# An attention and mixture-of-experts kernel: a new order for VectorE inside a unit, accumulators kept over the groups, and later stores of x from twelve buffers

## The chip, the cores and the metric

The kernel runs on one NeuronCore of a Trainium2 chip. The metric is the device time of one execution in microseconds. TensorE (PE) multiplies matrices into PSUM, VectorE (DVE) and ScalarE (ACT) read and write PSUM and SBUF, GpSimd (POOL) converts data and issues the loads of weights, and SyncE (SP) issues the other DMAs from one queue. Every engine takes its instructions in the order in which they were written and waits for the others through semaphores.

## What is computed

The first part is attention with a sliding window, for 8 batches of 576 positions and 8 heads of 64:

```python
scores = scale * np.matmul(q, k.transpose(0, 1, 3, 2))
mask = (rel >= 0) & (rel < 128)
scores = np.where(mask, scores + slopes * -np.abs(rel), -1e9)
attn = softmax(scores)
x = (attn @ v)            # as 4608 tokens of 512 values
```

The second part routes the 4608 tokens over 8 experts. Eight rounds of row and column normalization of exp(x @ w_gate) give a weight P for every token and expert, and every expert works on every token:

```python
for e in range(8):
    h = np.maximum(x @ w1[e], 0.0)          # 512 -> 1024
    out += P[:, e:e+1] * (h @ w2[e])        # 1024 -> 512
```

## The kernel before, in words

**Stage one** (to about 366 us) does the attention batch by batch, together with experts 0 and 1. A batch has five blocks of positions (four of 128, one of 64), and a block two steps of four heads. A step computes scores on TensorE, exponentials on ScalarE (`exps`, L429), the mask on VectorE (L442) and the weighted values on TensorE (`values`, L467); VectorE divides by the sum and writes half of a block of x into the tile `xsb` (L478). `turn_x` transposes the finished block, on TensorE for batches 0, 1, 2 and 7 (L498, copied out at L507 or L509) and by a DMA for the others (L511), and then stores the block to the DRAM tensor `xd` (L512), which stage two reads. The `xsb` tiles come from 3 buffers, which the converted tail of q and k (`turn_tail`) shares. The loads of v (`load_v`, L373), of the next batches' q and k (`load_qk`, L270) and the stores stand on SP's one queue in the order of the program. For batches 0 to 2, q and k are converted (L286, L288; L284 on GpSimd) and turned on TensorE in pairs of heads (`turn_pe`, L350). A filler weaves matmuls of experts 0 and 1 (L115 and L137) between the steps, so many per step as a backlog asks; their results go to the DRAM tensor `ysp`.

**Stage two** does experts 2 to 7 for 18 groups of 256 tokens. A unit is one expert for one group, 108 in all. Both matrix products are cut into 2x2 blocks. In most units the first product takes seven block products instead of eight, as Strassen's method does: TensorE runs the parts a11, s1, s2, a12, s3, s4, a22 (`part`, L957) into three PSUM banks A, B and C. ScalarE copies one bank into another between the parts (L1109, L1110, L1115), VectorE adds two pairs of sums, here called h3 (L1121) and h1 (L1125), and ScalarE applies the maximum with zero (`relu`, L970). Part a22 writes bank B again and so comes after h3 has read it. Part s1 reads T1, s2 reads T2, s3 reads T3 and a22 reads T4, which are sums of x blocks that VectorE makes one unit ahead (`sums_x`, L902 to L904) from the transposed tile `xset`. Expert 7, and the units before the fifth, take the plain first product (`l1_bank`, L937, L946).

The x of a unit is scaled by P two units ahead (`scale_x`, L878) and transposed by two DMAs on SP (`turn_xs`, L890) that land in `xset`.

The second product of unit n-1 runs inside unit n, between the parts of the first: seven products numbered 1 to 7 (`product`, L995), which need sums of h that VectorE makes at the head of unit n (`make_sums`, L974 to L976). They accumulate over the experts of a group in two PSUM tiles of two banks each: products 3, 4 and 5, 2 in the first, 6, 7 and 1 in the second. When a group's last expert is through, VectorE adds the products into the SBUF tile `acc` (`gather`, L1037): 3 and 4 as soon as they are done, 5 and 2 later in the same unit, and 6, 7 and 1 at the head of the next unit, whereupon `finish` (L1045) stores the output. The results of experts 0 and 1 of the next group are loaded into `y` (`load_y`, L1006) and start `acc` (`begin`, L1010 and L1013) three and four units into the group.

"First unit" below is the unit in which the old group's last products run, "second unit" is the next one.

## Time and profile before

| | us |
|---|---|
| median of 3 runs | 1111.12 (1110.44 to 1112.74) |
| the profiled execution | 1110.26 |
| its span | 1108.3 |
| TensorE busy | 1022.0 (92%) |
| VectorE busy | 768.7 (69%) |
| ScalarE busy | 557.0 (50%) |
| stores of x | 32 of 128 KB, 8 of 64 KB |

The rows of the profile read as follows. A row in order of time has its start, its length, the engine, the line of the kernel, the operation, output and inputs with their sizes and a count of merged instructions. In brackets stands the idle time of the engine before it and what ended that. PEld rows are loads of weights for the matmuls. A row of waits has the engine and line that waited, what it waited for, the total, how often and the longest. Busy time of TensorE is modelled at the ends of its matmuls.

### The profile page before, as it was taken

The numbers are of one execution on the slowest core, as the hardware profiler recorded it, in microseconds if no ns is written. First come the engines' busy times: TensorE is split into PE (matmuls) and PEld (weight loads), VectorE is DVE, ScalarE is ACT, GpSimd is POOL, SyncE is SP. The second block draws the span as 40 slices with busy tenths as digits, with TensorE's granted clock in tenths as the row PEclk, the third lists the DMA queues.
The fourth block names the chain that finished last, engine by engine and source line by source line (L and its number), as shares of the span: only waits on it lengthen the run. The fifth ranks groups of instructions, "written<-read, shape, count | busy, mean of one in ns | idle before, by whom it ended". The sixth has DMA issues, their size and how long they took to land.

```text
span 1108.3 us, 26671 instructions
## 1 busy us (share of the span) xinstructions
PE 1022.0 (92%) x11079; PEld 806.6 (73%) x11079; DVE 768.7 (69%) x1720; ACT 557.0 (50%) x973; POOL 80.8 (7%) x143
## 2 busy tenths in 40 slices
PE   6589899999999999999999899999999999989988
PEld 4344444444544789888889888888888988888977
DVE  4355565666578697776877776877776877777866
ACT  6346445554433345555555555555555555545543
POOL 1210323125110000000000000000000000000000
PEclk9699999999999999999999999999999999999999
DMA  9982787889997323324422432332332332342361
GB/s 250 208 221 56 197 180 197 187 216 178 225 188 143 91 49 86 82 51 81 93 62 66 89 77 50 87 77 54 82 77 52 90 78 54 87 78 49 87 115 30
DMA packets 264424, 122.37 MB, mean 110 GB/s; under 512 B 201968, under 2 KB 255728, under 8 KB 264304
## 3 DMA queue, kind: packets, MB, share of 16 engines
q1 hardware_dynamic: 249568, 102.68, 40.1%
q0 software_dynamic: 14304, 17.84, 9.7%
q8 instruction: 86, 1.41, 0.5%
q14 instruction: 34, 0.28, 0.1%
q10 hardware_dynamic: 432, 0.16, 0.1%
HBM read 78.30 MB, written 23.59 MB: 92 GB/s over the span
## 4 chain that ended last, share of the span: by engine, by line
PE 46%; DVE 27%; DMA 5%; ACT 5%; issue 4%; SPq 1%; DVEq 0%; ACTq 0%
PE psS_m L995 12%; PE psh L115 8%; PE psy L137 8%; PE psh L937 6%; DVE acc L1037 5%; PE psB L957 4%; DMA xset<-xs 4%; DVE hs L1121 4%; DVE hs L974 4%; ACT hs L970 4%; DVE hs L975 3%; DVE xs L878 3%; PE psA L957 2%; DVE xset L902 2%; PE psC L957 2%
## 5 line engine op out<-in xcount | busy, mean ns | idle before, releaser
L995 PEld LDWEIGHTS <-hs 128*128 128x128 f16 x2996 | 280.2, 98 | 49.6 <-issue 22.2
L957 PEld LDWEIGHTS <-w1l 128*128 128x128 f16 x2720 | 174.2, 98 | 37.7 <-issue 34.1
L970 ACT ACTIVATE hs<-hs 128x512 f16<-128x512 f16 x170 | 104.3, 630 | 189.3 <-DVE hs L1121 189.3
L995 PE MATMUL psS_m<-w2l,hs 128*128 128x256 f16 x1440 | 186.6, 273 | 1.1 <-DVE acc L1037 0.8
L974 DVE TENSOR_TENSOR hs<-hs 128x1024 f16<-128x1024 f16 x107 | 74.0, 691 | 133.5 <-ACT hs L970 80.3
L115 PE MATMUL psh<-xT,w1t 128*128 128x512 f16 (+1 forms) x608 | 142.3, 373 | 4.1 <-DVE xT L509 3.7
L137 PE MATMUL psy<-w2t,hT 128*128 128x512 f16 x576 | 136.0, 383 | 2.8 <-DVE xsb L478 2.8
L127 ACT ACTIVATE hT<-psh 128x512 f16<-128x512 f32 (+1 forms) x144 | 83.5, 586 | 107.9 <-PE psh L115 107.5
L995 PE MATMUL psS_m<-more,hs 128*128 128x256 f16 x864 | 119.3, 275 | 0.0
L957 PEld LDWEIGHTS <-s 128*128 128x128 f16 x1632 | 106.2, 98 | 3.2
L946 ACT ACTIVATE hs<-psh 128x512 f16<-128x512 f32 x92 | 54.9, 597 | 99.9 <-PE psh L937 97.6
L957 PE MATMUL psA<-xset,w1l 128*128 128x128 f16 x1360 | 104.6, 220 | 0.0
L137 PEld LDWEIGHTS <-hT 128*128 128x128 f16 x576 | 53.8, 98 | 64.8 <-issue 3.1
L115 PEld LDWEIGHTS <-w1t 128*128 128x128 f16 x608 | 55.6, 100 | 57.0 <-issue 8.7
L546 DVE CAST yo<-psy 128x512 f16<-128x512 f32 x68 | 46.8, 689 | 59.6 <-PE psy L137 58.8
L429 ACT ACTIVATE pt<-psS 128x1024 f16<-128x1024 f32 (+2 forms) x80 | 67.7, 852 | 37.4 <-PE psS L411 30.8
L957 PE MATMUL psB<-xset,s 128*128 128x128 f16 x1088 | 82.9, 219 | 0.0
L1115 ACT COPY psC<-psB 128x512 f32<-128x512 f32 x85 | 48.5, 571 | 59.8 <-PE psB L957 59.8
L957 PE MATMUL psB<-xset,w1l 128*128 128x128 f16 x680 | 52.1, 220 | 26.6 <-DVE hs L1121 26.5
L1037 DVE TENSOR_TENSOR acc<-acc,psS_m 128x256 f32<-128x256 f32 (+1 forms) x162 | 74.1, 504 | 3.4 <-PE psS_m L995 2.8
L442 DVE TENSOR_TENSOR pt<-pt,mask 128x1024 f16<-128x1024 f16 (+2 forms) x80 | 53.3, 666 | 32.4 <-ACT pt L429 32.2
L937 PE MATMUL psh<-xset,w1t 128*128 128x256 f16 x576 | 74.7, 273 | 0.0
(113 smaller groups left out, 1414.3 us busy)
## 6 DMA issues: line engine op xcount, KB each, us to landing
y<-ysp SPq DMA_DIRECT2D x36, 256.0 KB, 3.2
ysp<-yo SPq DMA_DIRECT2D x68, 128.0 KB, 3.0
v<-in_v_dram SPq DMA_DIRECT2D x32, 256.0 KB, 4.4
out_dram<-acc SPq DMA_DIRECT2D x31, 256.0 KB, 2.6
q<-in_q_dram SPq DMA_DIRECT2D x5, 1024.0 KB, 7.3
k<-in_k_dram SPq DMA_DIRECT2D x5, 1024.0 KB, 9.7
xtok<-xd SPq DMA_DIRECT2D x34, 128.0 KB, 2.2
w2t<-in_moe_w_dram POOLq DMA_DIRECT2D x4, 1024.0 KB, 11.1
```

The lines of the kernel that those rows point to most:

```text
L115: nc.tensor.matmul(out=ps[:, 0:nt], lhsT=w1ts[e][:, dt, P * ft : P * ft + P], rhs=xT[:, at : at + nb, dt, :], start=(dt == 0), stop=(dt == ...
L127: nc.scalar.activation(out=st["hT"][:, ft, 0:nt], in_=ps[:, 0:nt], func=AF.Relu)
L137: nc.tensor.matmul(out=ps, lhsT=st["hT"][:, ft, P * ms : P * ms + P], rhs=w2ts[e][:, ft, :], start=(ft == 0), stop=(ft == NFT - 1),)
L429: nc.scalar.activation(out=pt[0:nk, :, 0 : nk + nn], in_=ps[0:nk, :, :, 0 : nk + nn].rearrange("p a y n -> p (a y) n"), func=AF.Exp, scale ...
L442: nc.vector.tensor_tensor(out=pt[0:nk, :, 0:w], in0=pt[0:nk, :, 0:w], in1=mask[0:nk, hs, 0:w], op=ALU.mult)
L937: nc.tensor.matmul(out=ps[:, f, :], lhsT=W1L[e][:, dt, P * ft : P * ft + P], rhs=x[:, dt], start=(f == 0 and dt == 0), stop=(dt == NDT - 1 ...
L946: nc.scalar.activation(out=h[n][:, fh : fh + 2, j : j + 2, :].rearrange("p t f k -> p f t k"), in_=ps.rearrange("p f (t k) -> p f t k", t= ...
L957: nc.tensor.matmul(out=ps[:, j, :], lhsT=SL[e][w][:, k, P * j : P * j + P], rhs=xset[n % 2][:, x, P * k : P * k + P], start=(start and j = ...
L970: nc.scalar.activation(out=h[n][:, slot], in_=src, func=AF.Relu)
L974: nc.vector.tensor_tensor(out=t[:, 4:6], in0=t[:, 0:2], in1=t[:, 2:4], op=ALU.add)
L995: nc.tensor.matmul(out=Ms[g, bk][:, half, :], lhsT=h[n][:, LEFT[m], f, :], rhs=W2L[e][RIGHT[m]][:, f, :], start=(e == 2 and f == 0 and hal ...
L1037: nc.vector.tensor_tensor(out=a, in0=a, in1=p2, op=op)
```

## The change

In stage one, `xsb` has 12 buffers (`XSB`) instead of 3. `turn_x` no longer stores its block at once: it appends it to a list, and `keep_x(3)` stores the block of three turns before; the rest is stored after the last turn.

In stage two:
- The two accumulator tiles are made once and serve all groups (`Ms[bk]` instead of `Ms[g, bk]`).
- In a unit with seven parts, bank B is named before bank C, the copy of A into B stands ahead of part s1, and product 3 runs before s1, product 4 after it.
- VectorE makes `sums_x` after h3 and h1, no longer before them.
- In the first unit the gather of 5 and 2 comes after those sums, ahead of products 6 and 7 in the program.
- In the second unit products 6 and 7 are gathered after the sums of h, and product 1 only after h1.
- `finish` and `load_y` come at the end of the unit, behind `turn_xs` on SP's queue.

```diff
-    XPE, YO = 3, 6
+    XPE, YO, XSB = 3, 6, 12
...
-                xsbs[b, kb] = asb.tile([P, H, Dh], FP16, name=f"xsb_{b}_{kb}", tag="xsb", bufs=3)
+                xsbs[b, kb] = asb.tile([P, H, Dh], FP16, name=f"xsb_{b}_{kb}", tag="xsb", bufs=XSB)
...
+        kept: list = []
+
+        def keep_x(left=0):
+            while len(kept) > left:
+                blk, lo, nk, xsb = kept.pop(0)
+                nc.sync.dma_start(out=xd[blk, lo : lo + nk, :], in_=xsb[0:nk].rearrange("p h d -> p (h d)"))
...
-            nc.sync.dma_start(out=xd[blk, lo : lo + nk, :], in_=xsb[0:nk].rearrange("p h d -> p (h d)"))
+            kept.append((blk, lo, nk, xsb))
+            keep_x(3)
...
         turn_x(B - 1, NKB - 1)
+        keep_x()
...
-                if e == 2 and half == 0 and bk % 2 == 0:
-                    t = aps.tile([P, 2, 2, 2 * P], FP32, name=f"psS_m{g}_{bk}", tag="psS", bufs=2)
-                    Ms[g, bk], Ms[g, bk + 1] = t[:, 0], t[:, 1]
+                if not bk % 2 and bk not in Ms:
+                    t = aps.tile([P, 2, 2, 2 * P], FP32, name=f"psS_m{bk}", tag="psS", bufs=2)
+                    Ms[bk], Ms[bk + 1] = t[:, 0], t[:, 1]
...
         for n in range(N):
+            end = ends(n - 1)
+            done, late = late, ()
             if n > 0:
                 make_sums(n - 1)
-            if late:
-                gather(units[n - 2][0], *late)
-                finish(units[n - 2][0])
-                late = []
...
+            if done:
+                gather(units[n - 2][0], 6, 7)
             scale_x(n + 2)
-            if n > 0 and units[n - 1][1] == 2:
-                load_y(g)
...
                 part(n, pa, "a11", B11, True)
+                pb = bank(n, "B")
+                nc.scalar.copy(out=pb, in_=pa)
+                product(n - 1, 3)
                 pc = bank(n, "C")
                 part(n, pc, "s1", T1, True)
-                pb = bank(n, "B")
-                nc.scalar.copy(out=pb, in_=pa)
                 nc.scalar.copy(out=s5, in_=pc)
-                product(n - 1, 3, 4)
+                product(n - 1, 4)
                 if end:
                     gather(g, 3, 4)
...
                 part(n, pb, "s3", T3)
-                sums_x(n + 1)
                 nc.vector.tensor_tensor(out=h[n][:, 3], in0=pb, in1=s5, op=ALU.add)
                 relu(n, 3, h[n][:, 3])
                 part(n, pc, "s4", B22)
                 turn_xs(n + 2)
                 nc.vector.tensor_tensor(out=h[n][:, 1], in0=pc, in1=s5, op=ALU.add)
                 relu(n, 1, h[n][:, 1])
+                if done:
+                    gather(units[n - 2][0], 1)
+                sums_x(n + 1)
+                if end:
+                    gather(g, 5, 2)
                 product(n - 1, 6, 7)
                 part(n, pb, "a22", T4)
                 relu(n, 2, pb)
                 product(n - 1, 1)
-                if end:
-                    gather(g, 5, 2)
-                    late = (6, 7, 1)
...
+            if done:
+                finish(units[n - 2][0])
+            if n > 0 and units[n - 1][1] == 2:
+                load_y(g)
+            if end:
+                late = (6, 7, 1)
```

More of the change, by code (lines that the diff above doesn't have):

```diff
@@ L316, in turn_tail @@
         def turn_tail(b):
-            t16 = asb.tile([P, HD], FP16, name=f"t16_{b}", tag="xsb", bufs=3)
+            t16 = asb.tile([P, HD], FP16, name=f"t16_{b}", tag="xsb", bufs=XSB)
             nc.gpsimd.tensor_copy(out=t16, in_=tails.pop(b).rearrange("p h d -> p (h d)"))
@@ L990, in product @@
                 bk, half = BANK[m]
-                if e == 2 and half == 0 and bk % 2 == 0:
-                    t = aps.tile([P, 2, 2, 2 * P], FP32, name=f"psS_m{g}_{bk}", tag="psS", bufs=2)
-                    Ms[g, bk], Ms[g, bk + 1] = t[:, 0], t[:, 1]
+                if not bk % 2 and bk not in Ms:
+                    t = aps.tile([P, 2, 2, 2 * P], FP32, name=f"psS_m{bk}", tag="psS", bufs=2)
+                    Ms[bk], Ms[bk + 1] = t[:, 0], t[:, 1]
                 for f in range(NF2):
                     nc.tensor.matmul(
-                        out=Ms[g, bk][:, half, :],
+                        out=Ms[bk][:, half, :],
                         lhsT=h[n][:, LEFT[m], f, :],
@@ L1021, in gather @@
                 bk, half = BANK[m]
-                ps = Ms[g, bk][:, half, :]
+                ps = Ms[bk][:, half, :]
                 for lo, step, op in {
@@ L1082 @@
         xs[:] = [per.tile([P, HD], FP16, name=f"xs_{i}", tag="yo", bufs=YO) for i in range(4)]
-        late: list = []
+        late: tuple = ()
         for n in range(N):
             g = units[n - 1][0]
+            end = ends(n - 1)
+            done, late = late, ()
             if n > 0:
                 make_sums(n - 1)
-            if late:
-                gather(units[n - 2][0], *late)
-                finish(units[n - 2][0])
-                late = []
             some((4, 1, 0, 3, 2)[n] if n < 5 else 0)
@@ L1094 @@
                 quads_w1(units[n - 1][1])
+            if done:
+                gather(units[n - 2][0], 6, 7)
             scale_x(n + 2)
-            if n > 0 and units[n - 1][1] == 2:
-                load_y(g)
             if n > 0 and units[n - 1][1] in (4, 5):
                 begin(g, units[n - 1][1] - 4)
-            end = ends(n - 1)
             if strassen(n):
@@ L1130 @@
                 product(n - 1, 1)
-                if end:
-                    gather(g, 5, 2)
-                    late = (6, 7, 1)
-            else:
+            else:
+                if done:
+                    gather(units[n - 2][0], 1)
                 pairs = ((3, 4), (5, 2), (6, 7), (1,))
@@ L1140 @@
                         gather(g, *pairs[i])
-                    if i == 2:
-                        sums_x(n + 1)
                 turn_xs(n + 2)
-                if end:
-                    late = (6, 7, 1)
+                sums_x(n + 1)
+            if done:
+                finish(units[n - 2][0])
[3 more added lines that the diff above has]
+                late = (6, 7, 1)
             if n == N - E + 2:
```

## The prediction

> **What bounds the kernel now.** I read the page first, then busy time by stretches, then the list of waits, and only then the order of time where the long waits lie. The page's span, the stretches before and after 366 us (where the dense experts end), and three rows of waits (the two of TensorE are those after 430 us, the one of VectorE is of the whole span):

> ```profile
> span 1108.3 us, 26671 instructions
> ```
> ```profile
> 0.00:366.00 366.00, 331.35 (x2563) 170.47 (x2564) 214.41 (x494) 175.78 (x286) 79.97 (x142) 0.97 0.86 187
> 366.00:1108.30 742.30, 690.60 (x8518) 636.14 (x8515) 554.33 (x1226) 381.26 (x687) 0.87 (x1) 1.00 0.33 73
> ```
> ```profile
> PE psB L957 <- DVE hs L1121: 26.1, 41, 3.3
> PE psS_m L995 <- DVE acc L1037: 18.3, 17, 1.1
> ```
> ```profile
> DVE xsb L478 <- DMA xd<-xsb: 33.8, 6, 17.5
> ```

> The columns of the stretches are length, then busy time of PE, PEld, DVE, ACT and POOL. TensorE is busy 331.35 of 366.00 and 690.60 of 742.30 us, so it is the bound in both, and only its idle 34.7 and 51.7 us can be won. The 51.7 has two names: 41 waits of part a22 for the sum h3 (26.1 us), and 17 waits of 1.1 us, one at each change of group. The chain of waits names the same lines. In stage one VectorE waits for the store of an x block to free its buffer.

> **The x stores and the twelve buffers.** Rows picked from stage one in order of time, and two loads by their time to landing (issued between 20 and 30 us):

> ```profile
> 18.74 2.72 SPq L270 DMA_DIRECT2D k<-in_k_dram  x1
> 28.33 0.88 POOL L100 DMA_DIRECT2D w2t<-in_moe_w_dram  x1
> 29.55 1.19 SPq L512 DMA_DIRECT2D xd<-xsb  x1
> ...
> 39.82 0.61 POOL L383 CAST v<-v 128x512 f16<-128x512 f32 x1 [7.62 <-DMA v<-in_v_dram]
> 40.16 0.42 DVE L478 TENSOR_TENSOR xsb<-psN,rden 128x256 f16<-128x256 f32 x1 [17.50 <-DMA xd<-xsb]
> ...
> 50.10 0.81 PE L350 MATMUL psT<-ident,c 128*128 128x128 f16 x8
> 57.82 0.39 PE L467 MATMUL psN<-v,pt 128*128 128x65 f16 x7 [0.95 <-DVE pt L442]
> 59.14 1.04 PE L137 MATMUL psy<-w2t,hT 128*128 128x512 f16 x4
> ...
> 73.32 0.42 DVE L478 TENSOR_TENSOR xsb<-psN,rden 64x256 f16<-64x256 f32 x1 [2.14 <-DMA xd<-xsb]
> ...
> 127.09 3.54 PE L137 MATMUL psy<-w2t,hT 128*128 128x512 f16 x8 [2.79 <-DVE xsb L478]
> ...
> 148.16 1.89 PE L137 MATMUL psy<-w2t,hT 128*128 128x512 f16 x8
> ...
> 168.00 1.02 ACT L429 ACTIVATE pt<-psS 128x1024 f16<-128x1024 f32 x1
> 170.75 0.30 PE L467 MATMUL psN<-v,pt 128*128 128x65 f16 x4 [2.33 <-DVE pt L442]
> ```
> ```profile
> w2t<-in_moe_w_dram POOLq DMA_DIRECT2D x1, 1024.0 KB, 11.1
> k<-in_k_dram SPq DMA_DIRECT2D x1, 512.0 KB, 11.1
> ```

> With three buffers the fourth x block waits for the first block's store, which stands on SP's queue behind the loads of the next batch: VectorE stands 17.50 us, and everything behind it. With twelve the fourth block takes a fresh buffer; the store is issued three turns later, so v loads and the loads of batch 2 pass it on SP, and nothing waits for it.

> What is late next? The second half of k for batch 1: issued until 18.74 + 2.72 = 21.46, landing 11.1 later at 32.6; with its cast and copy (0.8) the third pair of turns can start at 33.4. Today it starts at 50.10: a gain of 16.7. The next loads are in time on that schedule: w2t lands at 28.33 + 0.88 + 11.1 = 40.3 and is first needed at 59.14 - 16.7 = 42.4; the second v block of batch 1 is cast at 39.82 (0.61 long), and the values that read it start at 57.82 - 16.7 = 41.1. Margins of 1 to 2 us, so I bound this term by 17.5 above and by 2 below (the DMA engines are full there, and only the three 128 KB stores leave the early queue: 384 KB at the stage's 187 GB/s, the last column above); I take 16.7, as the rows of the loads reach it.

> The other waits of this kind: 2.1 at 73.32. At 127.09 TensorE's 2.8, and eight matmuls that then took 3.54 instead of 1.89 (1.6 more): 4.4. At 170.75 TensorE waited 2.33, but ScalarE's exponentials came only at 168.00, so I take 1.0. After 180 us TensorE is busy throughout, and an advance is carried on. The same forty stores are issued on SP, the last three together behind the final turn. **Stage one: 16.7 + 2.1 + 4.4 + 1.0 = 24.2 us less.**

> **The order inside a unit.** One change of group today. The first unit of the new group still gathers products 3, 4, 5, 2 of the old one; the second gathers 6, 7, 1. Rows picked from the order of time, the last two from the unit after:

> ```profile
> 488.82 1.28 DVE L1037 TENSOR_TENSOR acc<-acc,psS_m 128x512 f32<-128x512 f32 x2
> 490.16 1.03 PE L995 MATMUL psS_m<-w2t,hs 128*128 128x256 f16 x8 [1.10 <-DVE acc L1037]
> ...
> 491.03 0.61 PE L957 MATMUL psB<-xset,s 128*128 128x128 f16 x8
> 491.74 0.69 DVE L1121 TENSOR_TENSOR hs<-psB,s5s 128x512 f16<-128x512 f32 x1 [0.65 <-PE psB L957]
> 492.35 0.68 DVE L1125 TENSOR_TENSOR hs<-psC,s5s 128x512 f16<-128x512 f32 x1
> 492.95 1.41 DVE L1037 TENSOR_TENSOR acc<-acc,psS_m 128x256 f32<-128x256 f32 x4
> 493.68 0.61 PE L957 MATMUL psA<-xset,w1l 128*128 128x128 f16 x8
> 494.27 0.69 DVE L974 TENSOR_TENSOR hs<-hs 128x1024 f16<-128x1024 f16 x1
> ...
> 497.32 0.61 DVE L878 TENSOR_SCALAR xs<-xtok,L_sb 128x512 f16<-128x512 f16 x2
> 497.85 0.42 DVE L902 TENSOR_TENSOR xset<-xset 128x512 f16<-128x512 f16 x1
> 498.10 1.04 PE L995 MATMUL psS_m<-w2l,hs 128*128 128x256 f16 x8
> 498.84 0.68 DVE L1121 TENSOR_TENSOR hs<-psB,s5s 128x512 f16<-128x512 f32 x1
> 499.57 0.61 PE L957 MATMUL psB<-xset,w1l 128*128 128x128 f16 x8 [0.43 <-DVE hs L1121]
> ...
> 505.18 0.42 DVE L902 TENSOR_TENSOR xset<-xset 128x512 f16<-128x512 f16 x1 [1.60 <-DMA xset<-xs]
> 506.98 0.61 PE L957 MATMUL psB<-xset,w1l 128*128 128x128 f16 x8 [1.07 <-DVE hs L1121]
> ```

> What it wins: the sums of x (497.85 to 498.84, 0.99 us, and at 505.18 a wait of 1.60 for a transpose) no longer stand before h3. Then h3 starts 0.71 after part s3 (491.03 to 491.74), before products 6 and 7 are through, and a22 never waits. The sums, now behind h1, are done before the next unit's T1 and T2 are read, and the transposes no longer stand behind two stores and two loads on SP. All 26.1 us go. A wait is longer than its bracket says: products 6 and 7 take 0.87, so 498.10 + 0.87 = 498.97, and a22 started at 499.57, 0.17 later than the 0.43 accounts for; times 41 that is 7.0. Two of the waits, the 3.3 of that row and one of 2.26, also halved the clock for a while (below, 1.6 each): 3.2. Together 36.3.

> What it does not win: the 18.3. In the built program product 5 still waits for the gather of 3 and 4, because both lie in one two-bank tile; keeping the tile over the groups changes its name and not that wait. The gather stands where it stood: 1.1 us times 17 stay.

> What it costs: two waits move onto the queue ahead of TensorE. In the built program product 3 of the new group waits for the last instruction of the gather of 5 and 2, and product 6 for the gather of 1. Today both are over in time. In the changed order:
> - The gather of 5 and 2 stands behind the sums: 492.95 + 0.99 = 493.94, plus 1.41 is 495.35. Product 3 now comes before s1, ready at 493.68 + 0.45 = 494.13, and starts 0.06 after the gather (490.10 to 490.16 above) at 495.41: a stall of 1.28.
> - Six blocks later (3, s1, 4, s2, a12, 5 and 2: 3.09) s3 starts at 498.50, h3 at 499.21, h1 at 499.82, the gather of 1 at 500.42, done after 0.64 at 501.06. Product 6 is ready at 499.39 and starts at 501.12: a stall of 1.73.

> TensorE works in order, so nothing behind these is done meanwhile. 3.01 us times 17 changes of group: 51.2. **Stage two: 51.2 - 36.3 = 14.9 us more.** From both sides: if a reused tile lets these products go at once, nothing is paid; if the clock falls, 27 more.

> The rest moves without cost: ScalarE's copy of psA goes ahead of that of psC (same count); stores of the output and loads of y go behind the transposes on SP, and y is read two units later.

> **Stalls and the clock.** Three rows of TensorE after stalls, and the granted clock (the number before the last two of the stretch) behind the second:

> ```profile
> 409.22 1.03 PE L995 MATMUL psS_m<-w2t,hs 128*128 128x256 f16 x8 [1.65 <-DVE acc L1037]
> ...
> 792.41 0.83 PE L957 MATMUL psB<-xset,w1l 128*128 128x128 f16 x8 [2.26 <-DVE hs L1121]
> ...
> 796.70 0.61 PE L957 MATMUL psB<-xset,s 128*128 128x128 f16 x8
> ```
> ```profile
> 793.50:795.00 1.50, 1.50 (x14) 1.38 (x13) 0.86 (x2) 0.61 (x3) 0.00 (x0) 0.50 0.00 0
> ```

> After 1.65 us of idling the matmuls kept their speed (eight in 1.03); after 2.26 the granted clock was 0.50, and a22 to s2 took 4.29 instead of the 2.66 that their blocks sum to: 1.6 lost. The new stall of 1.73 lies between, nearer to the harmless row, so I count nothing.

> [...]

> **The rivals.**
> - Slower: the clock. If the stall of 1.73 trips it, as the one of 2.26 did, each costs 1.6: at half of the changes of group 1101 + 14 = 1115, at all of them 1128. It decides from about 6 of 17 on. For it: two stalls in each such unit; against it: 1.65 was harmless.
> - Slower: the front is bound by its loads. If w2t or v come later than the rows say, the 16.7 shrinks towards 2: 1116. For it: POOL waited 7.62 for v at 39.82; against it: stores leave that queue.
> - The sums still wait for late transposes, and s1 waits where a22 did: half of the 36.3 remains, 1119.
> - The change does what its words say, and accumulators kept by bank free TensorE at the change of group: the 51.2 is not paid, 1050. The built program's waits speak against it.

> **How the numbers follow.** The profiled run took 1110.26, its span 1108.3 and 2.0 around it; that is 0.1% under the median of 1111.12. 1110.26 - 24.2 + 14.9 = 1101. Its own range is 1095 to 1108. Chances: this case 0.50, the clock 0.15, the front 0.12, late transposes 0.10, no stalls at the change of group 0.05, something else 0.08. For 8 in 10 the range runs from 1095 to 1120. Within 0.2% (2.2 us, about what three runs can tell, since they spread over 0.2%) I put 0.10; faster 0.56; slower 0.34.

> **What would show it.** Right: VectorE's wait for xd gone, the third pair of turns near 33 us and stage one over near 342; waits of psB gone; waits of psS_m grown from 18 to about 70 us, three at each change of group, of 1.1, 1.3 and 1.7; second units of 9.2 us and others of 6.2. Wrong: a granted clock below 1.00 behind the stalls, waits of PE for v or w2t before 60 us, waits of psC for the sums, or psS_m waiting no longer than today.

## The result, and the profile after

The changed kernel takes 1101.16 us (median of 4 runs) against 1110.84 us before, a ratio of 0.9918 with a 95% interval of 0.9892 to 0.9944: 0.8% faster. The forecast was 1101.0. The profiled execution took 1100.92 us, its span 1098.3, against 1110.26 and 1108.3.

The small difference is made of two large ones. Here are the two stages of the changed kernel (stretch, then busy time of PE, PEld, DVE, ACT and POOL, granted clock, DMA share, GB/s); stage two begins at 340.7 us, where its first matmul starts:

```profile
0.00:340.70 340.70, 326.64 (x2563) 168.51 (x2564) 212.65 (x494) 175.40 (x286) 78.08 (x142) 1.00 0.92 201
340.70:1098.30 757.60, 685.47 (x8517) 634.77 (x8515) 555.80 (x1226) 392.78 (x687) 0.88 (x1) 1.00 0.32 71
```

Before, stage two began at 366.1 us and lasted 742.2. So stage one is 25.4 us shorter and stage two 15.4 us longer; forecast were 24.2 and 14.9. (Ten traces below have the same first stage as the changed kernel; in them stage two begins between 339.8 and 344.3 us, so the 25.4 is known to a few us only.) TensorE was idle for 51.7 us of stage two before, and is for 72.1 now.

The list of waits, stage two alone (engine, line, what was waited for, total, times, longest):

```profile
PE psS_m L1004 <- DVE acc L1046: 66.4, 52, 1.9
```

No row of psB waiting for h3 is left: the 41 waits of 26.1 us are gone. Those of the products grew from 19.9 us in 18 waits, over the same stage, to 66.4 in 52, and there are three at each change of group instead of one. Here is one change of group in order of time, TensorE first (the last row is the next change of group), then VectorE:

```profile
467.29 1.03 PE L1004 MATMUL psS_m<-w2t,hs 128*128 128x256 f16 x8 [1.09 <-DVE acc L1046]
...
472.53 0.60 PE L1004 MATMUL psS_m<-more,hs 128*128 128x256 f16 x4 [1.11 <-DVE acc L1046]
...
478.27 1.03 PE L1004 MATMUL psS_m<-w2l,hs 128*128 128x256 f16 x8 [1.60 <-DVE acc L1046]
...
509.04 1.03 PE L1004 MATMUL psS_m<-w2t,hs 128*128 128x256 f16 x8 [1.09 <-DVE acc L1046]
```
```profile
470.86 0.29 DVE L913 TENSOR_TENSOR xset<-xset 128x256 f16<-128x256 f16 x1
471.07 1.41 DVE L1046 TENSOR_TENSOR acc<-acc,psS_m 128x256 f32<-128x256 f32 x4
...
476.94 0.68 DVE L1131 TENSOR_TENSOR hs<-psC,s5s 128x512 f16<-128x512 f32 x1
477.54 0.68 DVE L1046 TENSOR_TENSOR acc<-acc,psS_m 128x512 f32<-128x512 f32 x1
```

The three stalls are those of products 5, 3 and 6. Product 3 starts right behind the gather of 5 and 2 (471.07 + 1.41 = 472.48, start 472.53), which now stands behind the sums of x; product 6 starts right behind the gather of 1 (477.54 + 0.68 = 478.22, start 478.27), which stands behind h1. From one change of group to the next it is 509.04 - 467.29 = 41.75 us every time.

In stage one the gates' matmuls (x @ w_gate, L518 before and L526 after) make good marks, because the same sets come in the same places of both kernels. The kernel before, then the changed one, in order of time:

```profile
41.59 1.48 PE L248 MATMUL psJ<-ones 128*128 128x256 f16 x6
42.88 4.76 PE L115 MATMUL psh<-xT,w1t 128*128 128x256 f16 x32
...
60.25 0.54 PE L518 MATMUL psG<-wg_sb,xT 128*128 128x8 f16 x16
...
112.25 0.55 PE L518 MATMUL psG<-wg_sb,xT 128*128 128x8 f16 x16
...
132.53 1.02 PE L115 MATMUL psh<-xT,w1t 128*128 128x512 f16 x4 [0.54 <-DVE xT L509]
...
149.88 0.55 PE L518 MATMUL psG<-wg_sb,xT 128*128 128x8 f16 x16
...
171.57 1.89 PE L115 MATMUL psh<-xT,w1t 128*128 128x512 f16 x4
...
183.05 0.55 PE L518 MATMUL psG<-wg_sb,xT 128*128 128x8 f16 x16
...
216.82 0.55 PE L518 MATMUL psG<-wg_sb,xT 128*128 128x8 f16 x16
```
```profile
24.19 0.82 PE L248 MATMUL psJ<-ones 128*128 128x256 f16 x6
24.84 3.66 PE L115 MATMUL psh<-xT,w1t 128*128 128x256 f16 x32
...
31.20 0.61 PE L350 MATMUL psT<-ident,c 128*128 128x128 f16 x8
...
41.12 0.54 PE L526 MATMUL psG<-wg_sb,xT 128*128 128x8 f16 x16
...
91.00 0.55 PE L526 MATMUL psG<-wg_sb,xT 128*128 128x8 f16 x16
...
108.08 1.02 PE L115 MATMUL psh<-xT,w1t 128*128 128x512 f16 x4 [1.95 <-DVE xT L516]
...
125.43 0.55 PE L526 MATMUL psG<-wg_sb,xT 128*128 128x8 f16 x16
...
145.54 0.30 PE L467 MATMUL psN<-v,pt 128*128 128x65 f16 x4 [1.67 <-DVE pt L442]
...
156.64 0.55 PE L526 MATMUL psG<-wg_sb,xT 128*128 128x8 f16 x16
...
182.51 0.30 PE L467 MATMUL psN<-v,pt 128*128 128x65 f16 x4 [0.97 <-DVE pt L442]
...
191.55 0.55 PE L526 MATMUL psG<-wg_sb,xT 128*128 128x8 f16 x16
```

The lead of the changed kernel is 19.1 us at the first mark, 21.3 at the second, 24.5 at the third, 26.4 at the fourth (183.05 against 156.64) and 25.3 at the last: a new wait at 182.51 takes 1.1 back. (VectorE still has two waits for an x store in its list, 2.4 us in all, but at the tile yo.) Nothing waits for a store of x any more in front of the fourth block, and the third pair of turns starts at 31.20 instead of 50.10.

### The profile page after: what moved, and what is told of

Its sections match the earlier page's. It is cut to its first block, busy times and chain, and to the rows that moved or that the text cites. A ratio compares the mean times of both kernels' runs of the same rounds, so it can differ in the third digit from the quotient of the medians.

```text
span 1098.3 us, 26710 instructions
## 1 busy us (share of the span) xinstructions
PE 1012.1 (92%) x11079; PEld 803.3 (73%) x11079; DVE 768.4 (70%) x1720; ACT 568.2 (52%) x973; POOL 79.0 (7%) x143
## 3 DMA queue, kind: packets, MB, share of 16 engines
q8 instruction: 86, 1.41, 0.5%
## 4 chain that ended last, share of the span: by engine, by line
PE 65%; DVE 15%; issue 1%; ACT 1%; DMA 0%; DVEq 0%; SPq 0%
PE psS_m L1004 25%; PE psB L966 9%; PE psy L137 6%; PE psh L115 6%; PE psh L946 6%; DVE acc L1046 5%; PE psC L966 5%; PE psA L966 5%; DVE hs L1131 2%; DVE hs L1127 1%; DVE hs L983 1%; DVE hs L984 1%; DVE xs L887 1%; ACT hs L955 1%; DVE hs L985 1%
## 5 line engine op out<-in xcount | busy, mean ns | idle before, releaser
L1004 PEld LDWEIGHTS <-hs 128*128 128x128 f16 x2996 | 277.0, 98 | 97.8 <-issue 72.8
L1004 PE MATMUL psS_m<-more,hs 128*128 128x256 f16 x864 | 129.0, 273 | 18.8 <-DVE acc L1046 18.8
L983 DVE TENSOR_TENSOR hs<-hs 128x1024 f16<-128x1024 f16 x107 | 74.0, 691 | 101.0 <-ACT hs L955 53.6
L115 PE MATMUL psh<-xT,w1t 128*128 128x512 f16 (+1 forms) x608 | 139.7, 368 | 3.4 <-DVE xT L516 3.0
L137 PE MATMUL psy<-w2t,hT 128*128 128x512 f16 x576 | 134.3, 380 | 0.0
L1127 DVE TENSOR_TENSOR hs<-psB,s5s 128x512 f16<-128x512 f32 x85 | 58.8, 692 | 81.1 <-PE psB L966 79.8
L137 PEld LDWEIGHTS <-hT 128*128 128x128 f16 x576 | 53.5, 98 | 60.9 <-issue 1.5
L554 DVE CAST yo<-psy 128x512 f16<-128x512 f32 x68 | 46.9, 690 | 72.1 <-PE psy L137 59.8
L429 ACT ACTIVATE pt<-psS 128x1024 f16<-128x1024 f32 (+2 forms) x80 | 67.7, 852 | 30.0 <-PE psS L411 23.4
L984 DVE TENSOR_TENSOR hs<-hs 128x1024 f16<-128x1024 f16 x107 | 73.2, 684 | 0.0
L442 DVE TENSOR_TENSOR pt<-pt,mask 128x1024 f16<-128x1024 f16 (+2 forms) x80 | 50.0, 625 | 31.9 <-ACT pt L429 31.8
## 6 DMA issues: line engine op xcount, KB each, us to landing
q<-in_q_dram SPq DMA_DIRECT2D x5, 1024.0 KB, 7.0
k<-in_k_dram SPq DMA_DIRECT2D x5, 1024.0 KB, 9.4
w2t<-in_moe_w_dram POOLq DMA_DIRECT2D x4, 1024.0 KB, 10.4
```

Source lines behind the costliest of these rows:

```text
L115: nc.tensor.matmul(out=ps[:, 0:nt], lhsT=w1ts[e][:, dt, P * ft : P * ft + P], rhs=xT[:, at : at + nb, dt, :], start=(dt == 0), stop=(dt == ...
L137: nc.tensor.matmul(out=ps, lhsT=st["hT"][:, ft, P * ms : P * ms + P], rhs=w2ts[e][:, ft, :], start=(ft == 0), stop=(ft == NFT - 1),)
L429: nc.scalar.activation(out=pt[0:nk, :, 0 : nk + nn], in_=ps[0:nk, :, :, 0 : nk + nn].rearrange("p a y n -> p (a y) n"), func=AF.Exp, scale ...
L983: nc.vector.tensor_tensor(out=t[:, 4:6], in0=t[:, 0:2], in1=t[:, 2:4], op=ALU.add)
L984: nc.vector.tensor_tensor(out=t[:, 6:8], in0=t[:, 1:4:2], in1=t[:, 0:3:2], op=ALU.subtract)
L1004: nc.tensor.matmul(out=Ms[bk][:, half, :], lhsT=h[n][:, LEFT[m], f, :], rhs=W2L[e][RIGHT[m]][:, f, :], start=(e == 2 and f == 0 and half = ...
```

## The experiments

Ratios are to the kernel before, from runs beside it, with 95% intervals.

**The first part alone** (the kernel before with `XSB = 12`, `kept` and `keep_x`).

> The kernel before with the first part of the change alone: twelve buffers for the x blocks and their stores three turns later; the order inside a unit and the accumulators stay as before. Theory (VectorE's wait for the stores is what stage one loses, and it has nothing to do with stage two): the first matmul of stage two comes near 346 us as in the changed kernel, against 371.3 before, stage two keeps its 737 us, and the kernel takes 1110.3 - 25.4 = 1085 us. Rival (part of the 25 us comes from the other order in stage two, or is given back there because transfers of stage one now run into it): 1090 to 1108 us.

1084.25 us, 0.9767 (0.9748 to 0.9785). Stage two starts at 341.5 us and lasts 741.3. Expected was 1085: the first part is worth 26 us by itself.

**The second part alone:**

```diff
-    XPE, YO, XSB = 3, 6, 12
+    XPE, YO, XSB = 3, 6, 3
-            keep_x(3)
+            keep_x(0)
```

> The changed kernel with three buffers for the x blocks and each store issued at once, as before: the order inside a unit and the accumulators alone. Theory (two new stalls at each of 17 changes of group cost more than the 41 waits of psB give back): stage one ends where it ended before, at 371.3 us, stage two is 15.4 us longer than before, and the kernel takes 1110.3 + 15.4 = 1125.7 us; VectorE waits 17 us for xd again and the waits of psS_m stay near 66 us. Rival (the new order is a gain by itself): under 1108 us.

1126.1 us, 1.0142 (1.0123 to 1.0162): a loss of 1.4%. VectorE's wait for xd is back (15.03 us), stage two lasts 757.4 us, as in the changed kernel. The two parts do not touch each other: -26.1 and +15.8 make -10.3, and together they made -9.7.

**Twelve buffers, each store at once** (the kernel before with `bufs=12` alone).

> The kernel before with twelve buffers for the x blocks and nothing else: each store is issued at once, as before. Theory (what held VectorE was the fourth block's buffer; when the store is issued does not matter once nobody waits for it): third pair of turns of x near 31 us, stage one over near 346 us, 1085 us like the first part as a whole. Rival (a store on SP's queue holds up the transfers behind it, so the later stores are needed too): the third pair stays near 50 us or the loads come late, 1090 to 1110 us.

1086.18 us, 0.9776 (0.9757 to 0.9795). The third pair of turns starts at 31.52. The interval overlaps that of the first run: it is the buffers that win, and the later stores add nothing that shows. (Its stage two begins at 343.5 us, inside the spread of 339.8 to 344.3 with late stores.)

**One tile for each bank of the accumulators:**

```diff
-                if not bk % 2 and bk not in Ms:
-                    t = aps.tile([P, 2, 2, 2 * P], FP32, name=f"psS_m{bk}", tag="psS", bufs=2)
-                    Ms[bk], Ms[bk + 1] = t[:, 0], t[:, 1]
+                if bk not in Ms:
+                    Ms[bk] = mps.tile([P, 2, 2 * P], FP32, name=f"psS_m{bk}", tag="psM", bufs=4)
```

(`mps` is a pool of these four tiles; it takes the banks of the scores' psS, which gets a pool of its own here, closed after stage one.)

> The changed kernel with one tile for each accumulator bank instead of one for each pair of banks; same order of instructions. Theory (products 5, 3 and 6 wait for the gather of the other bank of their tile, whose numbers they do not overwrite): the three stalls at a change of group go, at most 0.65 us each is left at product 1, which does overwrite what the gather of 1 reads; a change of group costs 0 to 0.7 us instead of 4.3, so 1101 - 17 x 3.6 to 4.3 = 1028 to 1040 us, and the waits of psS_m fall from 66 to under 15 us. Rival (the waits are for the same bank, so the tile's size does not matter): 1095 to 1103 us with the waits near 66 us.

1037.6 us, 0.9345 (0.9328 to 0.9362). With the same order of instructions and the same arithmetic, 64 us of stage two are gone. Its waits, then the stretch, then the one stall that is left at a change of group:

```profile
PE psS_m L1007 <- DVE acc L1049: 8.0, 17, 0.6
```
```profile
342.90:1036.20 693.30, 679.99 (x8517) 633.56 (x8515) 552.75 (x1226) 390.91 (x687) 0.87 (x1) 1.00 0.36 78
```
```profile
470.29 0.60 PE L1007 MATMUL psS_m<-more,hs 128*128 128x256 f16 x4 [0.45 <-DVE acc L1049]
```

Products 5, 3 and 6 had waited for a gather that reads the other bank of their two-bank tile. Only product 1 now waits, for the gather that reads what it overwrites. Expected was 1028 to 1040.

**The old order on the same tiles** (the first run with the edit above).

> The run of the front alone (1084.25 us: twelve buffers, late stores, the old order inside a unit) with one tile for each accumulator bank. Theory (the old order loses to the pairs of banks only the wait of product 5, 1.1 us and 0.17 beside it at each of 17 changes of group, and keeps its 41 waits of psB): 1084.25 - 17 x 1.27 = 1063 us, waits of psB near 26 us as before. With the 1037.6 us of the new order on the same tiles that makes the new order a gain of 25 us once the tiles are single. Rival (the single tiles also take away what the sums of x wait for, so that the two orders come out alike): near 1040 us.

1072.07 us, 0.9664 (0.9635 to 0.9693); expected was 1063. Product 5 no longer waits, but of the 21.6 us (17 x 1.27) only 12 are won. The waits of a22 in stage two, the first run (pairs of banks) and then this one:

```profile
PE psB L966 <- DVE hs L1130: 27.5, 44, 3.3
```
```profile
PE psB L970 <- DVE hs L1133: 35.6, 49, 2.3
```

The missing 9 us went into these, 8.1 us more: product 5 started earlier, VectorE did not, and the next thing on TensorE's queue that needs VectorE waited in its place. So the new order is worth 1072.07 - 1037.6 = 34 us on single tiles, and costs 15 to 17 us on pairs.

**The two gathers put back** (the changed kernel, tiles of two banks):

```diff
             if done:
-                gather(units[n - 2][0], 6, 7)
+                gather(units[n - 2][0], 6, 7, 1)
...
-                if done:
-                    gather(units[n - 2][0], 1)
-                sums_x(n + 1)
                 if end:
                     gather(g, 5, 2)
+                sums_x(n + 1)
```

> The changed kernel, tiles of two banks, with two gathers put back: that of products 5 and 2 ahead of the sums of x in the first unit (the sums stay behind h1), those of 6, 7 and 1 together at the head of the second unit. Theory (what the new order costs is the place of these two gathers, what it wins is the place of the sums): product 3 waits some 0.3 us instead of 1.28, product 6 waits no more and a22 waits some 0.3 us through h3, product 5 keeps its 1.1 us: 1101 - 17 x 2.4 = 1060 us, waits of psS_m near 25 us. Rival (the gathers at the head of the second unit push h3 and h1 back so far that parts a22 and s4 wait as long as product 6 did): 1090 to 1101 us, with waits of psB.

1059.64 us, 0.9551 (0.9526 to 0.9575). Expected was 1060.

```profile
PE psS_m L1004 <- DVE acc L1046: 20.1, 18, 1.8
```

One stall for each change of group is left in the list, that of product 5. Two of 0.3 us, too short for it, show in the spacing of TensorE's rows: product 3 starts 0.73 behind a part that takes 0.44, and a22 starts 1.13 behind products that take 0.87. The place of these two gathers is what the second part costs, 42 us here.

**The sums of x alone** (the first run, with `sums_x(n + 1)` moved from ahead of h3 to behind h1, and nothing else; the edit is in every unit with seven parts, not in the first units alone).

> The run of the front alone (1084.25 us) with one further edit: in the first units the sums of x stand behind h1, as in the changed kernel; gathers, products, stores and loads stay in the old order. Theory (the place of the sums is the whole of the 36.3 us): the 41 waits of psB go, but the gathers of 6, 7 and 1 at the head of the second unit leave a22 some 0.3 us late at each of 17 changes of group: 1084.25 - 36.3 + 5 = 1053 us. Rival (the transposes of x still stand behind two stores and two loads on SP's queue, so that the sums and with them part s1 or a22 wait): 1060 to 1085 us, with VectorE waiting for xset longer than in the run with the gathers put back.

1063.25 us, 0.9596 (0.957 to 0.9621); expected was 1053. The waits of psB are gone altogether, also the 5 us that I had kept for a22, and no wait for transposes takes their place, though two stores and two loads still stand ahead of them on SP: VectorE waits for xset only twice in stage two, 1.6 us in all. What came instead, from TensorE's order of time:

```profile
463.42 1.03 PE L1004 MATMUL psS_m<-w2t,hs 128*128 128x256 f16 x8 [1.09 <-DVE acc L1046]
...
468.66 1.03 PE L1004 MATMUL psS_m<-more,hs 128*128 128x256 f16 x8 [0.66 <-DVE acc L1046]
```

Products 3 and 4, behind s1 in this order, wait for the gather of 5 and 2: 0.66 and the 0.17 beside it, 17 times, are 14 us, and 1084.25 - 36.3 + 14.1 = 1062. In the old order the sums ran in time that VectorE else spends waiting for part s3: with them ahead of h3 it still waited 0.65 us there, and now it waits 1.64. Behind h1 they push the gather of 5 and 2 back by 0.99 us, and the slack of product 3 becomes a stall, which my expectation had left out. The time lies in the rival's range, but not by the rival's cause.

**A longer stall** (the changed kernel, gather of 1 behind all three sums of x), and two of a length between (the gather behind the first sum, and behind the first two):

```diff
-                if done:
-                    gather(units[n - 2][0], 1)
                 sums_x(n + 1)
+                if done:
+                    gather(units[n - 2][0], 1)
```

> The changed kernel with the gather of product 1 behind the sums of x in the second unit, not ahead of them: the wait of product 6 grows by their 0.99 us, from 1.60 to about 2.6 us in the brackets, past the 2.26 us after which the clock was seen at 0.50 in the kernel before. If a stall of that length does not touch the clock: 1101 + 17 x 1.0 = 1118 us with a granted clock of 1.00 throughout. If it halves the clock as it did there, at 1.6 us each: up to 1101 + 17 x 2.6 = 1145 us, with a granted clock below 0.95 in stretches behind the stalls.

> The changed kernel with the gather of product 1 behind the first of the three sums of x (0.45 us): the wait of product 6 becomes 2.05 us in the brackets. Waits of 1.95 us left the clock alone and 2.26 us halved it, so this one lies between. If the clock stays: 1101.2 + 17 x 0.45 = 1109 us. If it halves as behind the 2.58 us, at 1.55 us each: 1135 us.

> The changed kernel with the gather of product 1 behind the first two of the three sums of x (0.77 us): the wait of product 6 becomes 2.37 us in the brackets, longer than the 2.26 us that halved the clock in the kernel before. Theory (every stall of that length halves the clock for the same while): 1101.2 + 17 x (0.77 + 1.55) = 1141 us. Rival (the 2.26 us was a single case, and only the 2.58 us of the longer stall does it each time): 1114 us.

| gather of 1 behind | bracket of product 6, us | stalls that halved the clock, in the trace | time, us | ratio to the kernel before |
|---|---|---|---|---|
| h1 (the change) | 1.60 | 0 of 17 | 1101.16 | 0.9918 |
| and one sum | 1.93 | 5 of 17 | 1115.27 (1105.89 to 1121.69, 10 runs) | 1.0038 (1.0005 to 1.0072) |
| and two sums | 2.26 | 13 of 17 | 1134.5 | 1.0253 (1.0216 to 1.0291) |
| and all three | 2.58 | 16 of 17 | 1143.53 | 1.0307 (1.0281 to 1.0334) |

(The last group's bracket is some 0.35 longer in each row. The second and third are 0.1 shorter than expected: the gather starts 0.33 behind a sum, while the next sum, which reads its result, starts after 0.45.) The longest stall in order of time, then the stretch behind it and the one that ends in it:

```profile
481.94 1.28 PE L1004 MATMUL psS_m<-w2l,hs 128*128 128x256 f16 x8 [2.58 <-DVE acc L1046]
483.02 1.06 PE L966 MATMUL psB<-xset,w1l 128*128 128x128 f16 x8
...
485.58 0.81 PE L1004 MATMUL psS_m<-more,hs 128*128 128x256 f16 x4
486.22 0.61 PE L966 MATMUL psC<-xset,s 128*128 128x128 f16 x8
```
```profile
482.60:486.00 3.40, 3.40 (x26) 2.91 (x24) 1.26 (x2) 0.72 (x2) 0.00 (x0) 0.50 0.93 308
478.60:482.00 3.40, 0.82 (x15) 0.69 (x13) 2.80 (x6) 1.23 (x2) 0.00 (x0) 1.00 0.38 77
```

Each halving cost 1.65 us: TensorE's busy time in stage two rose from 685.5 to 711.9, 26.4 for 16 of them. The case with one sum ran 10 times and spread over 16 us, ten halvings' worth; its mean granted clock was 0.998 in a run of 1107.44 us and 0.984 in that of 1121.69.

**No stall left** (the run with single tiles, and in the second unit):

```diff
-                gather(units[n - 2][0], 6, 7)
-            scale_x(n + 2)
+                gather(units[n - 2][0], 6, 7, 1)
+            if not (done and strassen(n)):
+                scale_x(n + 2)
...
-                turn_xs(n + 2)
+                if not done:
+                    turn_xs(n + 2)
...
                 if done:
-                    gather(units[n - 2][0], 1)
+                    scale_x(n + 2)
+                    turn_xs(n + 2)
```

> The run with one tile for each bank (1037.6 us) with the gather of product 1 at the head of the second unit, together with those of 6 and 7, and the scaling and transposing of x for two units later behind h1 in that unit. Theory (the last stall of a change of group, 0.45 us in the brackets and 0.17 beside it, is product 1 waiting for that gather, which now ends some 2.5 us earlier): no wait of psS_m, 1037.6 - 17 x 0.62 = 1027 us. Rival (with the gather ahead of h3 the stall moves to part a22 or s4, or the transposes come late for the sums): 1034 to 1040 us with waits of psB or psC in its place.

1026.75 us, 0.9258 (0.9232 to 0.9284), 7.4% under the kernel before. Its stage two is full:

```profile
342.80:1028.00 685.20, 679.49 (x8517) 632.41 (x8515) 554.27 (x1226) 389.35 (x687) 0.87 (x1) 1.00 0.38 79
```

TensorE works 679.49 of 685.20 us; its waits there sum to under 3 us. From here only fewer or shorter matmuls would make stage two shorter.

## Why the prediction was right, and where by luck

**Stage one, 24.2 forecast, 25.4 measured.** By the marks of the gates:

| term | forecast | measured |
|---|---|---|
| wait of 17.50 for the first block's store | 16.7 | 19.1 |
| wait at 73.32 | 2.1 | 2.1 |
| wait at 127.09 and half clock behind it | 4.4 | 3.2 |
| wait at 170.75, half clock behind it | 1.0 | 2.0 |
| a new wait, at 182.51 of the changed kernel | 0 | -1.1 |

The first term was mis-sized, and so was its upper bound of 17.5. The wait itself gave 17.4 (41.59 against 24.19), inside the bound; the other 1.7 are clock. Six matmuls took 1.29 us to the next row before and 0.65 now, and the 32 behind them 4.76 and 3.66: the clock was at half for the first of them, which I counted behind the wait at 127.09 and not behind this much longer one. And the limit that I named, the second half of k, was not one. The time to landing counts from the start of the issue, and I had added the issue's own 2.72 us to it. The store that VectorE waited for shows this: issued at 29.55 with 10.5 to landing, it is over at 40.05, and VectorE went on at 40.16, while 29.55 + 1.19 + 10.5 would be 41.24. So k was due at 18.74 + 11.1 = 29.8 and not at 32.6. In the changed kernel it was issued at 19.02 and cast at 29.96 with no wait, and the turns started at 31.20, not 33.4:

```profile
xd<-xsb SPq DMA_DIRECT2D x1, 128.0 KB, 10.5
```
```profile
19.02 1.62 SPq L270 DMA_DIRECT2D k<-in_k_dram  x1
...
29.96 0.62 ACT L288 CAST c<-k 128x512 f16<-128x512 f32 x1
```

The third term was too large because TensorE waits at that place again, 1.95 us for the copy of xT (108.08 above) where the same matmuls waited 0.54 before (132.53). The fourth was too small: the lead grew by 0.8 at the wait and by 1.2 behind it, since the clock was at half there too (0.50 from 171.5 to 174.7; four matmuls took 1.89 us at 171.57 instead of 1.04). And "an advance is carried on" did not hold for the 1.1 at 182.51. The errors cancel, which is luck. Two stretches of the kernel before, with the granted clock as the third number from the end:

```profile
41.00:42.80 1.80, 1.80 (x14) 1.34 (x14) 1.41 (x4) 0.59 (x1) 1.66 (x4) 0.50 0.61 161
42.90:44.90 2.00, 2.00 (x11) 1.40 (x10) 0.08 (x1) 0.38 (x1) 1.15 (x3) 0.50 0.94 173
```

**Stage two, 14.9 forecast, 15.4 measured.** Every step was found where the prediction put it:
- The waits of psB gone, 36.3: the run with the gathers put back has them gone too, and its stage two (715.6 us) is 742.2 - 36.3 and 9.7, which is 0.57 for each change of group, near the two stalls of 0.3 that were expected and found there. That the 0.17 beside each bracket and the clock belong to it holds: the brackets alone give 26.1.
- That the transposes had to pass the stores and loads on SP was no part of it: the sums alone won the same without that.
- Product 5 keeps its stall: 1.09 each time.
- Product 3, 1.28 forecast: 1.11 in the bracket and 0.17 beside it, 1.28. Product 6, 1.73 forecast: 1.60 and 0.17, 1.77. Times 17 that is 51.9 (forecast 51.2).
- No loss of clock at 1.73: none of 17 in the trace. (In two of the other three runs of the changed kernel the mean granted clock was 0.996, so it halved somewhere; no trace shows where.)

**The rivals.** That accumulators kept by bank free TensorE did not happen; what the words promise needs a tile for each bank, and then it is worth 64 us. The front was not bound by its loads, and the sums do not wait for transposes. The slower rival, the clock, was nearer than its 0.15 says: with product 6 waiting 0.33 us longer it halved at 5 changes of group, and with 0.66 at 13. Its price was right (1.6 forecast, 1.65 measured for each halving); that 1.73 lay on the harmless side was read off one row, and a gap of 0.6 us between two rows was all that there was to it. The reading was also uneven: 1.73 was a whole stall, the 1.65 of the harmless row a bracket, which with its 0.17 is 1.82. Measured alike, the new stall was the shorter one, and not between the two rows.

## What to carry to other kernels

Here a queue's wait went by the tile, not by the numbers in it: before an order is tuned, look which two things share a tile, since splitting it won 64 us where the new order alone lost 16. A stall that was taken away went to the next instruction that needed the same late engine (of 21.6 us 12 were won), so price a change of order by everything that then waits for the engine that is behind. Two parts of one change are worth pricing apart: here one was worth 25 us and the other cost 15, and the sum of 10 tells of neither.

## What the runs showed of the hardware

I had not expected that stalls of one length halve the clock in some cases and not in others. Three things show in the order of time. A halving lasted 3.4 us: in the run with the longest stall the matmuls' spacing puts its start at 482.60 (eight that take 0.87 at full speed took 1.08, 483.02 - 481.94, so the last 0.42 ran at half) and its end at 485.98. It did not start with the first matmul behind the stall: there 0.66 us after it, in another case of the 1.93 us run more than 1 us after it, as these rows of two changes of group of that run show:

```profile
651.23 1.03 PE L1007 MATMUL psS_m<-w2l,hs 128*128 128x256 f16 x8 [1.93 <-DVE acc L1049]
652.10 0.81 PE L969 MATMUL psB<-xset,w1l 128*128 128x128 f16 x8
652.71 1.06 PE L1007 MATMUL psS_m<-more,hs 128*128 128x256 f16 x4
```
```profile
952.41 1.59 PE L1007 MATMUL psS_m<-w2l,hs 128*128 128x256 f16 x8 [1.93 <-DVE acc L1049]
953.79 1.06 PE L969 MATMUL psB<-xset,w1l 128*128 128x128 f16 x8
```

And the starts lie on one grid: worked out in the same way they are at 652.38 (0.61 between 652.10 and 652.71 where 0.445 is full speed, so the last 0.33 at half) and at 952.77 (1.38 where 0.87 is full speed, so the last 1.02 at half), 300.39 us apart, which is 88.0 times 3.413. With the longest stall each change of group repeats after 44.38 us, 13.0 times 3.414, so once the stall fell badly it did so at every group after it. The record of the clock in the trace of the kernel before has four single halvings, each 3.41 us long, that start at 127.04, 171.42, 792.64 and 1079.36: 44.38, 621.22 and 286.72 us apart, which is 13.0, 182.0 and 84.0 times 3.413. By the grid of each trace the stalls that halved the clock in the three runs with longer stalls left 2.08 to 3.13 us idle inside one step of 3.413 us (bracket and 0.17), those of the same three runs that did not at most 2.10.

Two runs with the same stage two, the kernel before and the one with the buffers alone, tell the length of a stall from its place. The longest wait of a22 in each, and the stretch behind it:

```profile
1079.08 0.79 PE L957 MATMUL psB<-xset,w1l 128*128 128x128 f16 x8 [3.28 <-DVE hs L1121]
```
```profile
1079.40:1082.70 3.30, 3.30 (x29) 2.93 (x26) 2.08 (x5) 2.18 (x5) 0.00 (x0) 0.50 0.02 5
```
```profile
1055.29 0.61 PE L957 MATMUL psB<-xset,w1l 128*128 128x128 f16 x8 [3.11 <-DVE hs L1121]
```
```profile
1055.30:1058.70 3.40, 3.40 (x50) 3.26 (x50) 2.18 (x5) 2.75 (x6) 0.00 (x0) 1.00 0.02 5
```
